# Gated linear attention and a tanh-shrink MLP: the first unit's scans chunk by chunk, and w_in fetched tile by tile

## The chip, the cores and the metric

The kernel runs on one core of a Trainium2 chip. Its time is the device time of one execution in microseconds (us); of several runs the median counts. Five engines work side by side, each through its own instructions in order: TensorE (PE; its weight loads are listed apart as PEld), VectorE (DVE), ScalarE (ACT), GpSimd (POOL) and SyncE (SP), whose queue issues nearly all of the transfers here.

## The reference

```python
# q, k, v, alpha: (4, 8, 768, 48) float32, alpha in 0.8..1
state = np.zeros((B, H, D, D))
for t in range(S):
    state = alpha[:, :, t, :, None] * state + np.einsum('bhd,bhe->bhde', k[:, :, t], v[:, :, t])
    y[:, :, t] = np.einsum('bhd,bhde->bhe', q[:, :, t], state)
x = y.transpose(0, 2, 1, 3).reshape(3072, 384)
h = x @ w_in               # (384, 2048), float64
g = h - np.tanh(h)
out = g @ w_out            # (2048, 384), float64
```

The two weights are float64, 6.3 MB each.

## The kernel before

**Units and chunks.** Tokens are worked in 12 units of 256 (three for each of the four batches), a unit in two chunks of 128. The recurrence is taken in closed form inside a chunk: a scan U of the decays from the chunk's end backwards and a scan W forwards (lines 703 to 724) turn k into `kU` and q into `qW`, so that `scores` is a plain matmul (line 775), `masked` keeps its causal half (799), `products` multiplies with v and adds what the state carried over (831), and `features` copies the result to `xT` (866). `decay`, `back`, `natural`, `update` and `state` carry the state to the next chunk. In a unit's tiles the free dimension is laid out as blocks of 128 tokens plus one zero column, so one scan runs over all eight blocks (four head pairs times two chunks, 1032 columns) and starts afresh at each.

**Transposed inputs.** Channels have to lie on partitions. For unit 0 all of alpha, k and q, and for unit 1 k and q, are transposed by matmuls with the identity (`turn`, 648): `rough` is the loaded tile, `turned` the result in PSUM. Half a holds the even tokens, half b the odd ones; `place` (672) copies alpha's halves to `aT`, a on ACT and b on DVE, while `times` (675) multiplies k by U and q by W straight from PSUM. Later units are transposed on DVE (`flip`).

**PSUM.** There are eight banks: one tile of two banks named `sc` (`two_banks`, 530), two of one bank in `ps_h`, and four in `ps_o`. Before the change unit 0's alpha is turned into `sc`, k into two of `ps_o`, q into the two of `ps_h`. Unit 0's scores go to `sc` for chunk 0 and to the two of `ps_h` for chunk 1. A tile whose buffer is used again waits until all readers of its former contents are through.

**MLP.** Each unit runs eight steps. `first` is 12 matmuls of `w_in` with `xT` to `h`; ACT and DVE form g from it; `second` multiplies with `w_out`. Units 0 and 1 do it plainly (8 matmuls of 384 columns, line 1051); from unit 2 on seven products take the place of eight, on sums of the weights' blocks that `combine` makes once all weights are there (line 1066).

**Weights.** `w_in` and `w_out` come in eight pieces each of 768 KB (`fetch`, 548; `load_weight`, 39; `weight_parts`, 47) into a pool of four `raw` buffers, and are rounded there: two passes on ACT (lines 83 and 84), two on DVE (86 and 87). A piece of w_out is one transfer to 128 partitions. A piece of w_in has three row tiles j, and its rows are placed in four groups of partitions: 0 to 47, 64 to 111, and the 16-row groups 48 to 63 and 112 to 127. Each group is one transfer for all three j: 288, 288, 96 and 96 KB. Later every piece is read a second time, for a check of its range (`reload` and `look`, 977 and 980), through the same function.

**Order.** The order on each engine is not written by hand. `Planner` (319) lists the tasks with an estimated time, a rank and the tasks they follow, simulates several orders, and emits the best one. Every task in a `go`, `go_c` or `add` call is such an entry; its third argument is the estimate. SP's queue is one of the planned engines, so a transfer that has to wait holds up all those behind it. TensorE's free time up to `y 0.0` is filled with idle matmuls (`spin`, 1124).

Of the kernel before, what the change touches and what calls it, by code (L numbers as in the profile page):

```python
# [9 lines left out]
FP32 = mybir.dt.float32  # L10
# [7 lines left out]
P = 128  # L18
# [20 lines left out]
def load_weight(nc, pool, rows, **kw):  # L39

    raw = pool.tile([P, WN], I64 if rows[0][1].dtype != FP32 else FP32, name="raw", **kw)
    for at, src in rows:
        nc.sync.dma_start(out=raw[at].rearrange("p (j n) -> p j n", n=src.shape[-1]), in_=src)  # L43
    return raw


def weight_parts(w_in, w_out, pad_rows, what, s):

    if what == "out":
        return [(slice(0, P), w_out.rearrange("(j p) n -> p j n", p=P)[:, 2 * s:2 * s + 2, :])]  # L50
    parts = []
    for i in range(len(pad_rows[0])):
        at, f0 = pad_rows[0][i]
        step = pad_rows[1][i][1] - f0
        src = w_in[f0:f0 + len(pad_rows) * step].rearrange("(j p) n -> p j n", p=step)
        parts.append((at, src[0:at.stop - at.start, :, 2 * s * P:2 * (s + 1) * P]))
    return parts

# [363 lines left out]
def fast(tc, q, k, v, alpha, moe_w_in, moe_w_out, out, w_in, w_out, ident, ok, pad_rows):  # L422
# [17 lines left out]
    with ExitStack() as ctx:  # L440
# [165 lines left out]
        def gla(u, rank):  # L606
# [5 lines left out]
            m = {}  # L612

            direct = u == 0

# [5 lines left out]
            for what, name in enumerate(("aT", "kT", "qT", "v")):  # L621
                go(f"load {name}", "SP", 1.3 if direct or u == 1 and by_matmul(u, what) else 2.0, -9 + 0.1 * what,
                   [what < 3 and u > 0 and not by_matmul(u - 1, what) and not by_matmul(u, what) and f"{name}{prev}"]
                   + [u == 1 and (f"kUb 0" if what == 3 else "turn qTb 0")]
                   + [f"{last} {u - 2}.{CU - 1}" for last in ("y", "state") if what == 3 and u > 1
                      and (last == "y" or (u - 2) % UPB < UPB - 1)],
                   lambda what=what: load(u, what), lat=2.5)
# [15 lines left out]
            def new(name):  # L643
                m[name] = two.tile([P, NP, CU, P], FP32, name=name)
                return m[name]
            makes = (lambda: tail[:, :, 0:P].rearrange("p (g c) t -> p g c t", c=CU),
                     lambda: new("kT"), lambda: new("qT"))
            def turn(what, n):

                if what == (2 if u else 0):  # L650
                    if "both" not in m:
                        m["both"] = two_banks()
                    t = m["both"][:, n]
                elif what == 2:
                    t = ps_h.tile([P, NP, P], FP32, name="turned", tag="h")
                else:
                    t = ps_o.tile([P, NP, P], FP32, name="turned", tag=f"o{2 * u + n}")
                m["turned", what, n] = t
                for g in range(NP):
                    for r in range(2):  # L660
                        at = (head(g, r) * CU + n) * D
                        T.matmul(t[HP * r:HP * r + HP, g, :], lhsT=rough[u, what][:, at:at + HP], rhs=ident,
                                 start=True, stop=True)

            def turned(what, n):
                return m.pop(("turned", what, n)).rearrange("p g (c i) -> p g c i", c=CU)

            def each(x, n):

                return x.rearrange("p (g c) (i two) -> p g c i two", c=CU, two=2)[:, :, :, :, n]  # L670

            def place(n):
                (V.tensor_copy if n else A.copy)(each(tail[:, :, 0:P], n), turned(0, n))

            def times(what, by, n):
                name = ("aT", "kT", "qT")[what]
                if n == 0:
                    new(name)
                V.tensor_mul(each(m[name].rearrange("p g c t -> p (g c) t"), n), turned(what, n), each(m[by][:, :, 1:], n))

            later = u > 0
            for n, ab in enumerate("ab"):
                if by_matmul(u, 0):
                    go(f"turn aT{ab}", "PE", 1.1, n * 0.1, ["load aT", later and "masked 0.0"], lambda n=n: turn(0, n))
                    go(f"aT{ab}", "DVE" if n else "ACT", 0.65, 0, [f"turn aT{ab}"], lambda n=n: place(n))
                if by_matmul(u, 1):
                    go(f"turn kT{ab}", "PE", 1.1, 1 + n * 0.1,
                       ["load kT"] + [later and x for x in ("x 0.0", "y 0.1", "state 0.1")], lambda n=n: turn(1, n))
                    go(f"kU{ab}", "DVE", 0.72, 3, [f"turn kT{ab}", "U", n and "kUa", later and "back 0.1", later and "turn qTb"],
                       lambda n=n: times(1, "U", n))  # L690
                if by_matmul(u, 2):
                    go(f"turn qT{ab}", "PE", 1.1, 2 + n * 0.1,
                       ["load qT", later and f"aT{ab}" if by_matmul(u, 0) else "masked 0.0"], lambda n=n: turn(2, n))
                    go(f"qW{ab}", "DVE", 0.72, 5, [f"turn qT{ab}", "W", n and "qWa", later and "y 0.1", later and "turn kTb"],
                       lambda n=n: times(2, "W", n))
            for what, (name, k_) in enumerate((("aT", 0), ("kT", 2), ("qT", 4))):
# [5 lines left out]

            def scan_U():


                U = m["U"] = two.tile([P, N, P + 1], FP32, name="U", bufs=1)
                V.tensor_tensor_scan(out=U.rearrange("p n t -> p (n t)")[:, ::-1], data0=aT[:, :0:-1],  # L707
                                     data1=after[:, ::-1], initial=0.0, op0=ALU.mult, op1=ALU.add)

            def ends():  # L710
                U = m["U"]
                e = m["ends"] = two.tile([P, NP, CU], FP32, name="ends")
                e = e.rearrange("p g c -> p (g c)")
                V.tensor_tensor(out=e, in0=U[:, :, 0], in1=low, op=ALU.max)
                V.reciprocal(before[:, 0::P + 1], e)

            def shortest():
                V.tensor_reduce(out=least[:, u:u + 1], in_=m["U"][:, :, 0], axis=AX.X, op=ALU.min)

            def scan_W():  # L720

                W = m["W"] = two.tile([P, N, P + 1], FP32, name="W", bufs=1)
                V.tensor_tensor_scan(out=W.rearrange("p n t -> p (n t)"), data0=aT[:, 0:N * (P + 1)],  # L723
                                     data1=before, initial=0.0, op0=ALU.mult, op1=ALU.add)

# [13 lines left out]
            def done(by, what):  # L739

                return lambda u: [f"{by}{ab} {u}" for ab in "ab"] if by_matmul(u, what) else [f"{by} {u}"]
            kU, qW = done("kU", 1), done("qW", 2)
            go("U", "DVE", 2.3, 1, (["aTa", "aTb"] if by_matmul(u, 0) else ["aT"])
               + (kU(u - 1) + [f"sizeU{prev}", f"least{prev}"] if prev else []), scan_U)
            go("ends", "DVE", 0.4, 3, ["U"], ends)
            go("least", "DVE", 0.15, 7, ["U"], shortest)
            go("W", "DVE", 2.3, 3, ["ends"] + (qW(u - 1) + [f"sizeW{prev}"] if prev else []), scan_W)
            if not by_matmul(u, 1):
                go("kU", "DVE", 1.4 if halved(u) else 1.2, 3, ["kT", "U"], lambda: scale("kT", "U"))
            if not by_matmul(u, 2):  # L750
                go("qW", "DVE", 1.2, 5, ["qT", "W"], lambda: scale("qT", "W"))
            go("sizeU", "ACT", 1.3, 5, ["U"], lambda: size("U", 0))
            go("sizeW", "ACT", 1.3, 7, ["W"], lambda: size("W", 1))

# [8 lines left out]
            def chunk(c):  # L763
# [56 lines left out]
                def decay():  # L820
                    V.tensor_mul(old[0:ROWS, :, 0:D], old[0:ROWS, :, 0:D],
                                 m["ends"][0:ROWS, :, c:c + 1].to_broadcast([ROWS, NP, D]))

# [84 lines left out]
                if past and not (u == 0 and c == 1):  # L908
                    held = [f"masked {past}"]
                    if u > PLAIN or u == PLAIN and c:  # L910
                        held += [f"x {past}", not past_last and f"state {past}", not last and "natural"]
                go_c("scores", "PE", 1.0 if halved(u) else 1.2, 7, kU(u) + qW(u) + held, scores)
                go_c("masked", "DVE", 1.55 if halved(u) else 1.4, 8, ["scores", f"y 0.0" if u == 1 and c == 0 else past and u > 0 and f"y {past}"], masked)
                if n > 0:
                    go_c("decay", "DVE", 0.4, 6, [f"ends {u}", f"state {past}"], decay)
                if direct:
# [5 lines left out]
                if not last:  # L922
                    go_c("back", "PE", 0.5, 6, kU(u) + [past and not past_last and f"state {past}", u > 0 and c and f"x {past}",
                                                       u > PLAIN and f"x {past}", u == PLAIN and not c and f"masked {past}"], back)
# [309 lines left out]
```

## Time and profile before

| | |
|---|---|
| median of 6 runs | 592.37 us (591.69 to 599.26) |
| profiled execution | 598.15 us; its span 596.4 us, 1.75 us outside it |
| mean granted TensorE clock | 0.996 |
| TensorE busy | 575.6 us (97%), 6.9 of it idle matmuls before 18 us |
| DVE, ACT busy | 443.2 (74%), 321.8 us (54%) |
| first MLP matmul | at 27.78 us |
| first matmul of the seven-product form | near 143.7 us |
| bytes moved | 50.68 MB, about 16.7 of them in the first 74.6 us (five slices of 14.9 us at 189, 182, 228, 234 and 284 GB/s) |

Times inside the profile count from the span's start. Averages over the whole span mislead here: the first tenth is short of data, the rest is nearly solid TensorE work, so what a change does to the first 75 us and to the few later gaps decides.

### The profile page before, as it was taken

To read this page: it belongs to the slowest core of one execution; us is meant where nothing else is said; L and a number is where in the kernel's file an instruction comes from. 1 tells how busy PE (TensorE), PEld (TensorE's weight loads), DVE (VectorE), ACT (ScalarE), POOL (GpSimd) and SP (SyncE) were. 2 spreads that over 40 slices of the span, in tenths; PEclk is the share of its full clock that TensorE was granted. 3 is DMA by queue.
4 is the path that set the end of the run, shared out by engine and by line. 5 is a ranking of instruction groups with operands and counts; after the bars stand their busy time and mean duration, and the time that the engine had idled before them with its cause. 6 is when DMAs were issued, how large, how long until landed. Compare 5 with 4: busy or idle time off the path is not lost.

```text
span 596.4 us, 11389 instructions
## 1 busy us (share of the span) xinstructions
PE 575.6 (97%) x4431; PEld 505.5 (85%) x4431; DVE 443.2 (74%) x860; ACT 321.8 (54%) x565; POOL 5.8 (1%) x22
## 2 busy tenths in 40 slices
PE   7988899999998999999999999999999999999994
PEld 7876677778997989889899898898999898899994
DVE  5977689989866968968788788868678745634642
ACT  2576897637747657566666454445443333423430
POOL 3000000000000000000000000000000000000000
PEclk9999999999999999999999999999999999999998
DMA  9999952126465472546242131130010000000001
GB/s 189 182 228 234 284 113 71 36 60 161 82 130 138 96 178 82 111 119 145 82 119 81 35 78 29 36 78 28 27 35 1 27 8 1 29 8 0 27 0 34
DMA packets 60831, 50.68 MB, mean 85 GB/s; under 512 B 35904, under 2 KB 50528, under 8 KB 60768
## 3 DMA queue, kind: packets, MB, share of 16 engines
q1 hardware_dynamic: 57856, 48.88, 35.5%
q10 hardware_dynamic: 2912, 0.98, 0.8%
q8 instruction: 37, 0.61, 0.4%
q14 instruction: 26, 0.21, 0.1%
HBM read 44.04 MB, written 4.72 MB: 82 GB/s over the span
## 4 chain that ended last, share of the span: by engine, by line
PE 75%; DMA 13%; DVE 3%; ACT 3%; SPq 2%; issue 2%; ACTq 0%; DVEq 0%
PE h L1006 34%; PE o L1066 26%; PE o L1051 6%; DMA raw<-in_moe_w_in_dram 5%; PE sc L858 3%; DMA ar<-in_alpha_dram 3%; PE sc L796 3%; DMA vt<-in_v_dram 2%; PE sc L846 2%; DMA kr<-in_k_dram 1%; DMA raw<-in_moe_w_out_dram 1%; PE sc L897 1%; DMA qr<-in_q_dram 1%; PE sc L884 1%; SPq L43 1%
## 5 line engine op out<-in xcount | busy, mean ns | idle before, releaser
L1006 PE MATMUL h<-xT,w_in 128*128 128x256 f32 x1152 | 265.7, 380 | 2.3 <-DVE w_in L87 1.7
L1006 PEld LDWEIGHTS h<-xT,w_in 128*128 128x128 f32 x1152 | 215.0, 190 | 30.7 <-DVE w_in L87 2.1
L1015 ACT ACTIVATE u<-h 128x512 f32<-128x512 f32 x96 | 56.9, 593 | 167.5 <-PE h L1006 167.2
L1023 DVE TENSOR_TENSOR w<-h,u 128x512 f32<-128x512 f32 x96 | 66.0, 688 | 92.1 <-ACT u L1015 91.0
L1066 PE MATMUL o<-b,e 128*128 128x192 f32 x480 | 91.1, 326 | 0.0
L1066 PE MATMUL o<-w_out,e 128*128 128x192 f32 x320 | 81.2, 336 | 0.0
L1066 PEld LDWEIGHTS o<-b,e 128*128 128x128 f32 x480 | 80.2, 190 | 0.0
L1027 DVE SCALAR_TENSOR_TENSOR g<-z,w 128x512 f32<-128x512 f32 x96 | 65.7, 686 | 9.0 <-ACT z L1019 5.2
L1066 PE MATMUL o<-b,g 128*128 128x192 f32 x320 | 65.1, 326 | 0.0
L1019 ACT ACTIVATE z<-u 128x512 f32<-128x512 f32 x96 | 60.2, 628 | 2.3
L1066 PEld LDWEIGHTS o<-w_out,e 128*128 128x128 f32 x320 | 56.0, 190 | 4.6 <-issue 0.5
L1066 PEld LDWEIGHTS o<-b,g 128*128 128x128 f32 x320 | 54.2, 190 | 0.0
L1033 ACT ACTIVATE big<-u 128x1024 f32<-128x1024 f32 x48 | 50.3, 1048 | 0.1
L1051 PE MATMUL o<-w_out,g 128*128 128x384 f32 x128 | 44.3, 489 | 2.8 <-DVE g L1027 1.8
L1051 PEld LDWEIGHTS o<-w_out,g 128*128 128x128 f32 x128 | 23.9, 190 | 16.9 <-DVE g L1027 2.2
L1039 DVE TENSOR_TENSOR e<-g 128x256 f32<-128x256 f32 x80 | 33.3, 416 | 1.6
L1040 DVE TENSOR_TENSOR e<-g 128x256 f32<-128x256 f32 x80 | 33.2, 415 | 0.0
L818 DVE TENSOR_TENSOR pm<-sc,mask 64x256 f32<-64x256 f32 (+1 forms) x60 | 28.7, 505 | 3.3 <-PE sc L796 3.0
L707 DVE TENSOR_TENSOR_SCAN U<-aT,after 128x1032 f32<-128x1032 f32 x12 | 27.5, 2293 | 0.1
L723 DVE TENSOR_TENSOR_SCAN W<-aT,before 128x1032 f32<-128x1032 f32 x12 | 27.6, 2298 | 0.0
L83 ACT ACTIVATE more<-raw 128x768 int16<-128x768 uint32 x16 | 17.2, 1076 | 15.1 <-DMA raw<-in_moe_w_in_dram 9.0
L796 PEld LDWEIGHTS sc<-qT,kT 48*64 48x64 f32 x640 | 15.2, 133 | 9.6 <-issue 4.3
(126 smaller groups left out, 549.1 us busy)
## 6 DMA issues: line engine op xcount, KB each, us to landing
raw<-in_moe_w_out_dram SPq DMA_DIRECT2D x16, 768.0 KB, 6.4
raw<-in_moe_w_in_dram SPq DMA_DIRECT2D x32, 288.0 KB, 6.2
ar<-in_alpha_dram SPq DMA_DIRECT2D x44, 96.0 KB, 3.1
kr<-in_k_dram SPq DMA_DIRECT2D x40, 96.0 KB, 2.3
qr<-in_q_dram SPq DMA_DIRECT2D x40, 96.0 KB, 2.2
raw<-in_moe_w_in_dram SPq DMA_DIRECT2D x32, 96.0 KB, 5.8
vt<-in_v_dram SPq DMA_DIRECT2D x20, 96.0 KB, 2.6
vt<-in_v_dram SPq DMA_DIRECT2D x40, 48.0 KB, 2.6
```

The costliest lines, as they stand in the source:

```text
L796: T.matmul(sc[r][rows:rows + HP, g, HP * half:], lhsT=m["kT"][q, g, c, rows:rows + HP], rhs=m["qT"][q, g, c, HP * half:], start=True, stop ...
L818: V.tensor_mul(to, of, mask[rows, gs, ts].unsqueeze(1).to_broadcast(list(to.shape)))
L1006: T.matmul(h[:, a, :], lhsT=w_in[:, j, f * P:(f + 1) * P], rhs=xT[u][:, j, :], start=(j == 0), stop=(j == KT - 1))
L1015: A.activation(m["u", s], m["h", s], AF.Square, scale=W_SCALE ** -1.5)
L1019: A.activation(m["z", s], m["u", s], AF.Square, bias=QB, scale=QA * W_SCALE)
L1023: V.tensor_mul(m["w", s], m["h", s], m["u", s])
L1027: V.scalar_tensor_tensor(out=g.rearrange("p a c t -> p (a c t)"), in0=m["z", s], scalar=QK, in1=m["w", s], op0=ALU.add, op1=ALU.mult)
L1033: A.activation(big, m["us", s // 2].rearrange("p s t -> p (s t)"), AF.Relu, bias=-U_FAST, scale=W_SCALE, accum_out=over[:, n:n + 1])
L1039: V.tensor_add(e[:, 0:2, :], g[:, 0], g[:, 1])
L1040: V.tensor_sub(e[:, 2:4, :], g[:, :, 1, :], g[:, :, 0, :])
L1051: T.matmul(m["o"][c], lhsT=g[:, a, c, :], rhs=w_out[:, f, :], start=(f == 0), stop=(f == FT - 1))
L1066: T.matmul(o[n][:, i], lhsT=g_, rhs=w_, start=(s == 0 and (n, i) in ((0, 0), (1, 0), (2, 1), (3, 0))), stop=(s == FS - 1), skip_group_chec ...
```

## The change

**Scans by chunk, in unit 0 only.** `aT`, U, W, kT and qT lay their blocks chunk first (`gc`). Each of U, `ends` and W becomes two tasks, one for each chunk with half the columns, and each of `kU` and `qW` becomes four: half a or b of the tokens, chunk a or b. The scores of chunk 0 are listed after chunk a's parts alone. Units 1 to 11 keep one scan for both chunks.

**Banks.** Unit 0's alpha is turned into two single banks of `ps_o`, k into the two of `ps_h`, q into `sc`.

**Pieces of w_in.** The transfers to 48 partitions are cut by row tile: 0 to 47 and 64 to 111 for j = 0, the same for j = 1, for j = 2, and then the two 16-row transfers with all three j. That makes eight transfers of 96 KB for a piece, where there were four. It holds for the fetch and for the reload. The planner's estimates for these tasks stay as they were (4.1 and 1.0 us on SP).

```diff
-        parts.append((at, src[0:at.stop - at.start, :, 2 * s * P:2 * (s + 1) * P]))
-    return parts
+        src = src[0:at.stop - at.start, :, 2 * s * P:2 * (s + 1) * P]
+        few = at.stop - at.start < 32
+        parts += [(0, at, slice(0, len(pad_rows)), src)] if few else [(j - 9, at, slice(j, j + 1), src[:, j:j + 1]) for j in range(len(pad_rows))]
+    return [x[1:] for x in sorted(parts, key=lambda x: (x[0], x[1].start))]
...
+            parted = u == 0
+            parts = [(x, slice(c * NP, (c + 1) * NP), slice(c, c + 1)) for c, x in enumerate("ab")] if parted else [("", slice(0, N), slice(0, CU))]
...
-                if what == (2 if u else 0):
+                if what == 2:
                     t = m["both"][:, n]
-                elif what == 2:
+                elif what == 1 and u == 0:
                     t = ps_h.tile([P, NP, P], FP32, name="turned", tag="h")
                 else:
                     t = ps_o.tile([P, NP, P], FP32, name="turned", tag=f"o{2 * u + n}")
...
-                    go(f"kU{ab}", "DVE", 0.72, 3, [f"turn kT{ab}", "U", ...
+                    for x, _, cs in parts:
+                        go(f"kU{ab}{x}", "DVE", 0.42 if x else 0.72, 3, [f"turn kT{ab}", f"U{x}", ...
...
-            def scan_U():
+            def scan_U(ns):
+                a, z = ns.start * (P + 1), ns.stop * (P + 1)
+                V.tensor_tensor_scan(out=m["U"][:, ns].rearrange("p n t -> p (n t)")[:, ::-1], data0=aT[:, z:a:-1],
+                                     data1=after[:, a:z][:, ::-1], initial=0.0, op0=ALU.mult, op1=ALU.add)
...
+            for x, ns, _ in parts:
+                go(f"U{x}", "DVE", 1.2 if x else 2.3, 1, (["aTa", "aTb"] if by_matmul(u, 0) else ["aT"]) ...
+                go(f"ends{x}", "DVE", 0.4, 3, [f"U{x}"], lambda ns=ns: ends(ns))
+                go(f"W{x}", "DVE", 1.2 if x else 2.3, 3, [f"ends{x}"] + ...
...
-                go_c("scores", "PE", 1.0 if halved(u) else 1.2, 7, kU(u) + qW(u) + held, scores)
+                go_c("scores", "PE", 1.0 if halved(u) else 1.2, 7, kU(u, c) + qW(u, c) + held, scores)
```

## The prediction

> **What bounds the kernel now.** I read the page's engine shares and slices first, then a table of stretches, TensorE's waits, the chain up to 70 us, and the instructions of the first 30 us.
>
> ```profile
> PE 575.6 (97%) x4431; PEld 505.5 (85%) x4431; DVE 443.2 (74%) x860; ACT 321.8 (54%) x565; POOL 5.8 (1%) x22
> DMA  9999952126465472546242131130010000000001
> ```
>
> TensorE is the bound of the whole, but the transfer engines are full for the first five slices (75 us). A change helps only where TensorE stands still.
>
> ```profile
> 30.00:40.00 10.00, 9.35 (x81) 7.28 (x82) 7.20 (x13) 6.79 (x10) 0.00 (x0) 1.00 1.04 214
> 40.00:50.00 10.00, 7.12 (x65) 5.02 (x66) 6.09 (x11) 8.79 (x13) 0.00 (x0) 1.00 1.07 246
> ...
> 60.00:70.00 10.00, 8.18 (x32) 5.66 (x31) 6.57 (x10) 8.44 (x12) 0.00 (x0) 1.00 1.04 305
> ```
>
> Columns: stretch, length, busy us of PE, PEld, DVE, ACT, POOL, granted clock, transfer share, GB/s. TensorE loses 0.65 + 2.88 + 1.82 = 5.35 us here, with transfers at 1.04 or more. Its waits by name:
>
> ```profile
> PE o L1051 <- DVE g L1027: 1.8, 1, 1.8
> PE h L1006 <- DVE w_in L87: 1.7, 1, 1.7
> PE o L1051 <- DVE w_out L87: 1.0, 1, 1.0
> PE h L1006 <- DVE w L1023: 0.6, 1, 0.6
> ```
>
> Those are 5.1 of the 5.35 us. 2.7 wait for a rounded weight outright; the 1.8 (at 66.18) stand behind a rounding too, as the chain shows:
>
> ```profile
> 13.01 6.48 DMA raw<-in_moe_w_in_dram
> ...
> 22.28 7.45 DMA raw<-in_moe_w_in_dram
> ...
> 32.73 9.99 DMA raw<-in_moe_w_in_dram
> ...
> 43.23 10.84 DMA ar<-in_alpha_dram
> ...
> 54.14 8.32 DMA raw<-in_moe_w_out_dram
> ...
> 63.49 1.05 ACT more L84
> ```
>
> From 13 to 63 us one transfer releases the next: SP issues only when an earlier one has landed. By the issues' own landings it is always the eighth before (issue 13.90, landing 13.88; 14.26, 14.23; 40.41, 40.40; 41.62, 41.60). Eight are in flight at most, so the rate of the transfers sets the pace.
>
> Later gaps are 1.95 us (180 to 200), 1.29 (220 to 240) and 1.05 (240 to 280). The end from 280 us is solid.
>
> **Part 1, alpha's banks.**
>
> ```profile
> 8.61 0.64 ACT L673 COPY aT<-sc 128x512 f32<-128x512 f32 x1 [3.58 <-PE sc L662]
> 9.28 0.69 DVE L673 COPY aT<-sc 128x512 f32<-128x512 f32 x1 [4.50 <-ACT aT L673]
> ```
>
> The turns of both halves take 5.56 to 8.50; ACT's copy of half a starts only after both, DVE's of b after ACT's. With a bank each, a can be copied after its own 16 matmuls, 7.0 (half of the 2.94 us) to 7.9, and ends by 8.6. So b starts at 8.6, whether or not it still waits for a: 0.7 us off DVE's start of U.
>
> **Part 2, scans by chunk.** DVE works without a break from 9.28 to the end of chunk 1's mask at 21.8 (including 1.5 us for rounding w_in's first piece, 17.85 to 19.40). Extra instructions in unit 0: one scan more for U and for W, two for `ends` (0.16 + 0.20 us), two products more each for kU and qW. The halves of the 2.30 us scan cost 0.06 (smallest memset) to 0.2 more each: 0.1 to 0.4. A product of 256 columns starts every 0.34 us (L1039) where one of 512 starts every 0.61: 4 x (0.68 - 0.61) = 0.3; by the 0.505 us of the mask's 256 columns from PSUM against 0.675 it is 4 x 0.335 = 1.3. `ends` adds 0.36. Sum 0.8 to 2.1; I take 1.0, since L1039 is the same shape.
>
> What it should buy is chunk 0's scores before chunk 1's scans. But q's turned halves now lie in `sc`, which has one buffer, and scores 0.0 goes to `sc`: it waits for chunk 1's qW after all. The four scans, `ends`, kU and qW, about 8.5 us of DVE, therefore come first: 9.28 - 0.7 + 8.5 + the extra, near 18, as now (17.94). Then masks, TensorE's products (y 0.1 ends at 25.2) and the first MLP matmul follow as before. So part 1 and 2 together: -0.7 + 1.0 = +0.3, and -1.5 if w_in's rounding falls behind the masks, where it is hidden by y 0.1. Bounds -1.9 (with extra 0.3) to +1.4; I take -0.4.
>
> **Part 3, the pieces.** Price of an issue: median 0.426 us, so a w_in piece costs SP 8 x 0.43 = 3.4 instead of 1.7 us; eight fetches add 13.6 us before 68 us, eight reloads as much up to 270. Behind them in SP's queue stand w_out's fetches, unit 1's k, q and v and later alpha, k, q. Closing entries of a transfer are 4-byte packets of 18 ns: 64 more a piece over 16 engines is 0.1 us.
>
> What it may gain is the rate. The packet records before 70 us: w_in's 2 KB packets take 182 ns (median), w_out's 3 KB packets 142, and w_out alone (65.7 to 67.6) runs at 400 GB/s. In the undisturbed reload of 147.86 the 48-row transfers land at 151.94 and 153.73: 295 KB in 1.79 us, 165 GB/s. Its first hundred packets take about 90 ns, then 170 to 240. So w_in is slow by where its rows lie, in SBUF or in HBM; the trace can't say which. Upper and lower rows in turn help if it is SBUF's side, and not if it is HBM's stride.
>
> [...]
>
> Bounds by rows: no gain (a piece spans 5.5 to 6.6 us early), or 3.4 us, where issuing becomes the limit (98 KB each 0.426 us is 231 GB/s); a w_out piece takes 2.0. I take 4, nearer the second, since 96 KB transfers of q land 2.0 us after issue on an idle queue (200.52 to 202.53), well within the 3.4 us that eight in flight allow. Fetch pairs start every (58.49 - 36.62)/3 = 7.3 us now and about 5.5 to 6 then, so by the sixth pair weights come some 8 us early. TensorE can't use more than it loses, 5.35. Next late is ACT, which rounds (2.1 us a piece) and makes u and z: busy 8.79 and 8.44 of ten us already. I take 3.2 of 5.35; bounds 0 and 5.35.
>
> In the reload the last landing comes 6.9 us after the first issue (147.86 to 154.73); then 7 x 0.43 + 2.0 to 2.2, near 5.2. What is queued behind is issued 1.7 us later but shares the engines with less. The later gaps (4.3 us) wait on such loads, through ACT: I take 0, bounds -2 and +3.
>
> **Sum.** -0.4 - 3.2 + 0 = -3.6 us: 598.15 becomes 594.55 for the profiled execution. That execution lies 5.8 above the median of the runs; taking the difference over, 592.37 - 3.6 = 588.8. This likeliest case spans 585.5 to 591.
>
> **Rivals.** *The transfers open up wholly:* all 5.35 us, rounding behind the masks (-1.9), and 1 to 2 of the later gaps: -8.3 to -9.3, 583 to 584. For it: the chain from 13 to 63 us is transfers alone. Against it: ACT's 8.79, and an order planned by estimates that the change leaves alone. 0.22.
>
> *Part 3 does not do what it says:* the rate is HBM's, 2 KB rows at a pitch of 16 KB; only -0.4 +- 1.5 is left, 590.5 to 593.5. For it: the 16-row transfers, on far fewer partitions, land 0.57 and 0.43 us apart, 172 to 228 GB/s, not slower. Against it: those overlap with the wide ones' end. 0.16.
>
> *Slower: the eight in flight.* A w_in piece now fills all eight places by itself, where two pieces and a w_out fitted. If a piece still takes 5.9 us, and w_out's 2.0 no longer overlap, the pair takes 7.9, with one landing (2.0) laid bare 9.3 instead of 7.3: 5 to 16 us later over eight pairs, of which TensorE's plain steps, tied to each piece, lose about 7: 599. It decides once a pair takes over 7.3 us. For it: the loaded queue makes even 96 KB take 10.84 us (43.23). Against it: that transfer stood behind two w_out pieces. 0.12.
>
> **How the numbers follow.** Forecast 0.50, rivals 0.22, 0.16 and 0.12. A measurement can tell about 1% from no change: 586.4 and 598.3. Below 586.4 lie the first rival and 0.08 of the forecast's own 0.50: 0.30. Above 598.3 lies most of the last, 0.09. The rest is 0.61. The range 583.5 to 593 leaves out a third of the first rival and nearly all of the last, about 0.19.
>
> **What would show it.** In the changed profile: DVE's copy of alpha at 8.6; scores 0.0 after the last qW, near 18; w_in packets near 100 to 130 ns instead of 182 and pairs every 5.5 to 6 us; TensorE's waits for `w_in L87` and `w_out L87` mostly gone before 66 us, ACT at 9 of ten there. Wrong would be: packets still at 180 ns, scores 0.0 well before 17 us, or new TensorE gaps behind late k, q or alpha after 130 us, where SP's queue is longer.

## The result and the profile after

| | before | after |
|---|---|---|
| median of the runs | 595.20 us (83 runs, 590.29 to 602.21) | 592.98 us (41 runs, 590.92 to 596.46) |
| ratio, 95% interval | | 0.9973 [0.9961, 0.9986] |
| profiled run, its span | 598.15, 596.4 us | 591.46, 589.6 us |
| first MLP matmul | 27.78 us | 27.77 us |
| TensorE idle, 20 to 70 us | 5.35 us | 1.62 us |

The change makes the kernel 0.27% faster, 1.6 us; 3.6 us, 0.6%, was forecast. The ratio is that of the means, over the fast runs of each kernel alone (those within 1.5% of its fastest, 76 of the 83 and all 41), so it is not the quotient of the two medians. The median of the kernel before moved too, from 592.37 us in the six runs shown to 595.20 in 83, so the ratio counts and not the difference from 592.37. The two profiled runs are 6.7 us apart, three times the difference of the medians: one execution each says little about a difference of this size.

First the page of the changed kernel: TensorE's line of busy times, then the transfers' share in 40 slices.

```profile
PE 573.4 (97%) x4425; PEld 504.3 (86%) x4425; DVE 443.4 (75%) x868; ACT 321.9 (55%) x565; POOL 5.8 (1%) x22
DMA  8899852043463433443342120220010000000001
```

TensorE's work is the same. The transfers are no longer full in the first slices. The stretches of ten microseconds, in the columns explained in the prediction:

```profile
30.00:40.00 10.00, 8.78 (x71) 7.25 (x71) 8.33 (x14) 8.59 (x13) 0.00 (x0) 1.00 0.90 220
40.00:50.00 10.00, 9.74 (x102) 7.34 (x100) 9.21 (x16) 8.60 (x14) 0.00 (x0) 1.00 1.01 282
...
60.00:70.00 10.00, 10.00 (x40) 7.41 (x39) 8.29 (x14) 9.24 (x14) 0.00 (x0) 1.00 0.95 320
```

The holes of 2.88 us (40 to 50) and 1.82 us (60 to 70) have shrunk to 0.26 and 0. The stretch from 30 to 40 got worse, 1.22 us for 0.65, and ScalarE (ACT) is at 8.6 to 9.2 of ten. TensorE's waits, each with its total, number and longest:

```profile
PE sc L816 <- ACT kn L908: 2.4, 2, 1.8
...
PE sc L808 <- DVE qT L687: 1.5, 1, 1.5
PE h L1026 <- DVE w L1043: 1.2, 1, 1.2
...
PE h L1026 <- DVE w_in L90: 0.3, 1, 0.3
```

Waits for a rounded weight fell from 2.7 us to 0.3. What is left stands behind ACT: `kn` and, through `u`, `w`. The chain shows the same (start, length, what):

```profile
21.39 5.59 DMA raw<-in_moe_w_in_dram
...
29.02 2.84 DMA raw<-in_moe_w_in_dram
...
32.92 1.05 ACT more L87
33.98 1.00 ACT junk L752 x2
34.98 0.48 ACT u L1035
...
39.45 3.54 DMA raw<-in_moe_w_in_dram
...
50.67 2.79 PE h L1026 x12
```

Before, transfers led the chain until 63 us. Now the last one in this part ends at 43, and from 46 us the chain is TensorE's own. Between 32.9 and 35.5 three passes of ACT stand in it one behind another; they matter below.

The start, from the instructions of ACT, DVE and TensorE:

```profile
6.95 0.63 ACT L678 COPY aT<-turned 128x512 f32<-128x512 f32 x1 [1.92 <-PE turned L671]
7.84 0.70 DVE L678 COPY aT<-turned 128x512 f32<-128x512 f32 x1 [3.06 <-PE turned L671]
16.46 1.16 PE L808 MATMUL sc<-qT,kT 48*128 48x128 f32 x16 [1.53 <-DVE qT L687]
```

DVE takes its half of alpha up when TensorE has turned it, no longer after ACT: 1.44 us earlier. The first scores still wait for chunk 1's last qW, as forecast, and start 1.5 us earlier than before. Nothing of this is left at 27.77, the first MLP matmul.

### The profile page after: what moved, and what is told of

Read it like the earlier page. It is cut to its first block, busy times and chain, and to the rows that moved or that the text cites. A ratio compares the mean times of both kernels' runs of the same rounds, so it can differ in the third digit from the quotient of the medians.

```text
span 589.6 us, 11492 instructions
## 1 busy us (share of the span) xinstructions
PE 573.4 (97%) x4425; PEld 504.3 (86%) x4425; DVE 443.4 (75%) x868; ACT 321.9 (55%) x565; POOL 5.8 (1%) x22
## 4 chain that ended last, share of the span: by engine, by line
PE 82%; DMA 5%; DVE 5%; ACT 4%; issue 2%; SPq 1%; POOL 0%; ACTq 0%; DVEq 0%; POOLq 0%
PE h L1026 37%; PE o L1086 27%; PE o L1071 7%; PE sc L878 3%; PE sc L816 3%; DMA raw<-in_moe_w_in_dram 2%; PE sc L866 2%; DMA ar<-in_alpha_dram 1%; PE sc L917 1%; DVE U L719 1%; PE sc L904 1%; DMA vt<-in_v_dram 1%; PE spin L1148 1%; ACT u L1035 1%; ACT junk L752 1%
## 5 line engine op out<-in xcount | busy, mean ns | idle before, releaser
L738 DVE TENSOR_TENSOR_SCAN W<-aT,before 128x1032 f32<-128x1032 f32 (+1 forms) x13 | 27.7, 2133 | 0.0
L719 DVE TENSOR_TENSOR_SCAN U<-aT,after 128x1032 f32<-128x1032 f32 (+1 forms) x13 | 27.6, 2133 | 0.1
L639 ACT COPY ar<-ar 32x512 f32<-32x512 f32 x22 | 13.5, 616 | 21.0 <-DMA ar<-in_alpha_dram 13.4
```

Of the source, the lines that this page charges most:

```text
L719: V.tensor_tensor_scan(out=m["U"][:, ns].rearrange("p n t -> p (n t)")[:, ::-1], data0=aT[:, z:a:-1], data1=after[:, a:z][:, ::-1], initia ...
```

## The experiments

They ran in three batches, each on one chip beside 35 runs of the kernel before (medians 595.83, 597.09 and 594.45 us). Ratios go against the batch's own; medians are of 12 runs. The two repeats of the kernel before, as a load of its own, show what ratios can tell:

**The kernel before, again (batches 1 and 3).** No edit.

> The kernel before, unchanged, as its own control: ratio 1.000 with an interval of about 0.002 to each side. Its profile is a second execution of the same program. If the 6.8 us between the two profiled spans (596.4 and 589.6) were all the change's, this span is near 596; if much of it is the scatter of executions (590.3 to 602.2 us before), the span lies elsewhere, and the trace shows at which time from the start the two executions of one program part.

> The kernel before as its own control, a second time: by chance alone 1.000 within 0.002. Together with the first control (0.9978) it tells how far a ratio here can be off through the load of the program, beyond its interval.

Measured: 593.84 us, 0.9978 [0.9952, 1.0003], and 596.02 us, 1.0007 [0.9972, 1.0043]. Two loads of one program have differed by 0.2% from the runs beside them. TensorE's idle time from 20 to 70 us was 3.75 and 4.01 us: the 5.35 of the profile that the prediction started from is the highest of three.

**The changed kernel, again (batches 2 and 3).** No edit.

> The changed kernel, unchanged. Its profile gives a second execution. Reading so far: in every profile a stretch of 3.41 us in which TensorE stood still for 1.97 us or more was followed by one at half clock (1.7 us lost), and none with 1.60 or less; and the changed kernel's median granted clock over its runs (0.993 to 0.994) is lower than that of the kernel before (0.996). Theory (the changed order gathers TensorE's slack in the gaps near 35 and 213 us, and these cost clock in part of the executions): median clock 0.992 to 0.995 again, below that of before on the same chip, and where this profile shows half clock away from the end, it follows the gap near 35 or near 213 us. At equal clock the kernel is 3 to 4 us faster than before, in the median 1.5 to 3: ratio 0.995 to 0.998. Rival (the clock is scatter and tells nothing): same median clock as before.

> The changed kernel, a third time. Its ratio has been 0.9973 and 0.9933. Theory: median clock 0.992 to 0.995, ratio 0.993 to 0.998; half clock in the profile, if any, after the gap near 35 or near 214 us.

Measured: 593.68 us, 0.9933 [0.9902, 0.9964], and 592.77 us, 0.9943 [0.9917, 0.9970]. With 0.9973 that makes a gain of 0.3 to 0.7% in three measurements: the sign holds in each, but the size moves by 0.4 points, somewhat more than between the repeats above (0.3). The median clocks, 0.993 and 0.9945, are as expected and below those of the kernel before in the same batches (0.995 and 0.996); the ratio of 0.9933 is a little below the 0.995 to 0.998 expected of it. In the first of the two profiles the clock falls after the gaps near 35 and 214 us, after stretches with 1.54 and 1.75 us of idle time, less than the 1.97 read until then; in the second it does not fall inside the work.

**Pieces alone, and the scans and banks alone (batch 1).** The first is the kernel before with the changed `load_weight` and `weight_parts`, the second the changed kernel with the old two:

```diff
...
-        parts.append((at, src[0:at.stop - at.start, :, 2 * s * P:2 * (s + 1) * P]))
-    return parts
+        src = src[0:at.stop - at.start, :, 2 * s * P:2 * (s + 1) * P]
+        few = at.stop - at.start < 32
+        parts += [(0, at, slice(0, len(pad_rows)), src)] if few else [(j - 9, at, slice(j, j + 1), src[:, j:j + 1]) for j in range(len(pad_rows))]
+    return [x[1:] for x in sorted(parts, key=lambda x: (x[0], x[1].start))]
```

> The kernel before with part 3 alone: w_in's pieces in eight transfers, upper and lower rows in turn. The planner's order is that of before. Theory (all of the gain is the pieces' rate, and TensorE's wait between 20 and 70 us is what it can buy): packets of w_in near 115 ns instead of 182, TensorE's lost time from 20 to 70 us from 5.35 to about 1.6 us, as in the changed kernel, and a ratio of 0.994 to 0.998. Rival (the scans and the new order bring the gain): ratio 0.999 to 1.002 though the packets are fast. Rival (the pieces gain more and the new order gives some back): ratio under 0.994.

> The changed kernel with w_in's pieces as before: parts 1 and 2 alone, in the changed planner's order. Theory (all of the gain is the pieces'): packets at 180 ns, y 0.1 ends about 1 us earlier than 25.2, first MLP matmul still near 27.8, ratio 0.999 to 1.001. Rival (scans and order bring the gain): ratio 0.996 to 0.998. Rival (they give some back): ratio 1.002 to 1.005.

Measured: 593.73 us, 0.9950 [0.9917, 0.9983], and 595.50 us, 0.9984 [0.9948, 1.0019]. The pieces alone give what the whole change gives, with 2.16 us of idle time from 20 to 70 (1.6 expected); the scans and banks give nothing that can be told from the repeats. What the scans and banks do when weights come slowly is seen in the second kernel's stretches:

```profile
30.00:40.00 10.00, 6.52 (x42) 5.47 (x41) 6.35 (x12) 7.93 (x12) 0.00 (x0) 0.95 1.01 207
40.00:50.00 10.00, 10.00 (x89) 7.45 (x88) 7.60 (x14) 8.92 (x14) 0.00 (x0) 0.88 1.06 235
```

The holes at 40 and 60 us are gone, and one of 3.48 us stands near 35: the planned order asks for the first MLP step's `w` sooner, and it comes later. Right behind it the granted clock falls to 0.95 and 0.88 (of the stretch).

**The same eight transfers, not in turn (batch 1).** The kernel of the pieces alone, with the same sizes, the same number of issues and the same rows of HBM; the three upper transfers first, then the three lower:

```diff
-[(j - 9, at, slice(j, j + 1), ...
+[(at.start - 999, at, slice(j, j + 1), ...
```

> As the pieces alone, with eight transfers of 96 KB, but the three of the upper rows first and then the three of the lower ones. Size, number of issues and the stride in HBM are those of the pieces alone; only the turn is missing. If the rate is limited by which rows of SBUF are written at one time: packets stay near 170 to 180 ns, a piece spans 5 to 6.5 us, ratio 1.000 to 1.006 (the extra issues cost and nothing is gained). If it was the size of a transfer, or the stride in HBM, that made them slow: packets near 115 ns and the ratio of the pieces alone.

Measured: 599.71 us, 1.0062 [1.0032, 1.0092]. The median of w_in's 2 KB packets before 70 us was 182 ns before (180 and 168 in its repeats), 196 with the old pieces under the new scans, 160 here, and 113 (changed) and 127 (pieces alone) in turn; in all nine profiles with the turn it is 109 to 127. So the smaller transfer explains less here (182 to 160 ns) than the turn of upper and lower rows of SBUF (160 to 127). Its stretches:

```profile
40.00:50.00 10.00, 6.93 (x57) 4.70 (x54) 5.90 (x10) 7.74 (x13) 0.00 (x0) 0.95 1.01 221
180.00:200.00 20.00, 17.03 (x133) 14.49 (x126) 14.00 (x30) 14.22 (x27) 0.00 (x0) 0.83 0.52 133
```

TensorE idles 3.07 us from 40 to 50 and 2.97 in one stop near 187, and the granted clock is down to 0.95 and 0.83 of these stretches. Against the pieces in turn, which differ in nothing else, this kernel is 1.1% slower. Against the kernel before it is 3.7 us slower, but not because its weights come later: w_in's eighth piece lands at 65.7 us (65.6, 64.3 and 63.6 in three profiles of before), and TensorE's idle time from 20 us on is 8.2 us (9.6, 6.3 and 7.6 before). What differs is the clock: 0.9909 by the mean of its 12 runs, 0.9955 in the 35 of the kernel before beside them. Of 594 us that difference is 2.7 us by estimate, most of the 3.7.

**Pieces and banks (batches 2 and 3).** Pieces, and the bank mapping, on the kernel before; scans whole, the planner's order of before:

```diff
-                if what == (2 if u else 0):
+                if what == 2:
...
-                elif what == 2:
+                elif what == 1 and u == 0:
```

> The kernel before with the pieces and the banks, without the scans by chunk; the planner's order is that of before. By the theory that the new order costs clock and the pieces give the time: median clock as before (0.996), alpha's copy on DVE at 7.9 to 8.6 instead of 9.28, ratio 0.993 to 0.996, below the changed kernel on the same chip. Rival (the scans by chunk are worth their cost): ratio above that of the changed kernel by 0.001 or more.

> The pieces and the banks in the order of before, once more. Two loads of one program have differed by 0.002 here, so this shows whether 0.992 holds: by the theory (pieces 3 to 4 us, no clock lost) 0.991 to 0.996 and a median clock of 0.996 or more, not above the changed kernel on the same chip.

Measured: 593.08 us, 0.9919 [0.9891, 0.9948], and 594.11 us, 0.9981 [0.9945, 1.0017]. Beside the changed kernel in the same batches (593.68 and 592.77) it is once 0.6 us less, once 1.3 more: no difference. The cut of the scans can't be seen in the time. The second load missed what was expected of it in all three points: the ratio is above 0.996, the median clock 0.9945, and it is slower than the changed kernel beside it. Its interval holds 1, so by itself it shows no gain.

**The scores' bank set free (batch 2).** The changed kernel, with unit 0's alpha and q turned into `ps_h` and k into `ps_o`, so that scores 0.0 need not wait for chunk 1's qW:

```diff
-                if what == 2:
+                if what == 2 and u > 0:
...
-                elif what == 1 and u == 0:
+                elif what != 1 and u == 0:
```

> The changed kernel, but unit 0's q is turned into the two banks of ps_h (after alpha, which goes there too) and k into two of ps_o, so that sc is free for chunk 0's scores. Same planner's order. If q's halves in sc hold chunk 0's scores back, as the prediction said: scores 0.0 start near 15.2 instead of 16.46 us and the gap of 1.53 us before them goes, y 0.1 ends about 1 us earlier than 24.3. Theory on the total: the plain steps wait for weights and for DVE near 35 us anyhow, so little of that 1 us reaches the end: ratio within 0.002 of the changed kernel on the same chip. Rival (the start sets the end): 0.002 lower.

Measured: 593.19 us, 0.9947 [0.9919, 0.9975], no more than the change itself. TensorE's instructions with a wait:

```profile
15.90 1.16 PE L808 MATMUL sc<-qT,kT 48*128 48x128 f32 x16 [0.19 <-DVE qT L687]
25.21 0.66 PE L671 MATMUL turned<-ident,rough 128*64 128x128 f32 x8 [0.55 <-DMA rough<-in_k_dram]
26.34 1.53 PE L671 MATMUL turned<-ident,rough 128*64 128x128 f32 x24 [0.48 <-DMA rough<-in_k_dram]
38.94 1.62 PE L1026 MATMUL h<-xT,w_in 128*128 128x256 f32 x3 [3.33 <-DVE w L1043]
```

The wait of 1.53 us is gone, and scores 0.0 starts at 15.90, 0.56 us earlier than in the changed kernel and not the 1.3 expected; y 0.1 ends 0.55 earlier (23.79). The next thing is late at once: unit 1's k arrives 1.03 us after TensorE wants it, the first MLP matmul comes at 28.68 and not at 27.77, and the wait for `w` near 35 us grows to 3.33.

**Eight idle matmuls near 35 us (batch 2).** The changed kernel, with TensorE kept at work ahead of the gap near 35 us:

```diff
+                    if u == 0 and s == 2:
+                        warm = ps_o.tile([P, P], FP32, name="warm", tag="o0")
+                        for _ in range(8):
+                            T.matmul(warm, lhsT=ident, rhs=ident, start=True, stop=True)
```

> The changed kernel with eight idle matmuls (about 1.1 us) into an unused bank ahead of unit 0's third first step, where TensorE stands still near 35 us. They add nothing to the output. If that gap costs clock in part of the executions: median clock up by 0.001 to 0.002, time down by 0.5 to 1.5 us against the changed kernel on the same chip. If the half clock comes from the gap near 213 us alone, or the clock tells nothing: no difference, within 0.001.

Measured: 593.05 us, 0.9929 [0.9903, 0.9955]. In the profile the full clock was kept near 35 us, where a gap of 1.28 us is left (another of 1.01 near 25 waits for unit 1's k), but it was lost for 3.41 us after a gap of 2.26 near 216. The median clock is 0.9955, for 0.993 of the changed kernel beside it, and 6 of 12 runs reach 0.996, for 2 of 12: the clock rose as expected, and a little more. The time, 593.05 for 593.68, is lower by as much as expected (0.5 to 1.5), but that is within the scatter of 12 runs: the gain is not shown, and one gap of two was covered.

**Reload in four transfers (batch 3).** Pieces and banks, with the eight transfers in the fetch alone:

```diff
...
-        few = at.stop - at.start < 32
+        few = whole or at.stop - at.start < 32
...
-    return [x[1:] for x in sorted(parts, key=lambda x: (x[0], x[1].start))]
+    return [x[1:] for x in sorted(parts, key=lambda x: (x[0], x[1].stop - x[1].start < 32, x[1].start))]
...
-            looked[n] = load_weight(nc, combo_pool[0], weight_parts(moe_w_in, moe_w_out, pad_rows, *pieces[n]))
+            looked[n] = load_weight(nc, combo_pool[0], weight_parts(moe_w_in, moe_w_out, pad_rows, *pieces[n], whole=True))
```

> The pieces and the banks in the order of before, but the second reading of the weights in four transfers a piece, as before. Prediction's step: the second reading was put at 0 with bounds -2 and +3 us. If that holds, the ratio is that of the pieces and banks on the same chip within 0.002, and TensorE's gaps from 180 to 270 us are as large as with eight (1.65, 0.97 and 0.96 us). If SP's eight issues delay the loads behind them: lower by 0.002 to 0.005, gaps smaller. If the faster second reading helps: higher by as much.

Measured: 595.01 us, 1.0005 [0.9973, 1.0037], against 0.9981 with both: within the scatter of a repeat, so the reload's share is not settled beyond that. The later gaps, 1.44, 0.57 and 0.78 us, are smaller than with eight transfers, though the ratio is higher: the two signs point to different rivals. A lone reload lands 6.1 us after its first issue in the changed kernel (146.62 to 152.69), 6.9 before; 5.2 was forecast.

## Why the forecast was half wrong

The forecast time, 588.8 us, is 4.2 below the 592.98 measured, and 2.8 of that is the base: 592.37 was the median of six runs, 595.20 is that of 83. That 592.98 still lies just inside the range of 583.5 to 593 is luck. What the theory has to answer for is the gain: 3.6 us forecast, 1.6 measured here, 4.0 and 3.4 by the ratios of the two repeats.

**The mechanism of part 3 was right.** Packets of 113 ns were in the band of 100 to 130; a piece takes 4.3 to 5.3 us from its first packet to its last (4 forecast, 5.4 to 6.7 before); waits for a rounded weight are nearly gone, and ACT is at nine of ten, as forecast. Too hopeful was the pace: from the third w_in piece to the eighth, last landings come every 6.5 us ((60.8 - 28.5)/5) where it was 7.2 ((65.6 - 29.7)/5), not 5.5 to 6 (the other profiles: 7.0 and 6.6 after, 7.0 and 6.9 before). The eighth comes at 60.8, 63.1 and 61.3 us in the three profiles of after, at 65.6, 64.3 and 63.6 in the three of before: 2.8 us early by the means, not 8. That was still enough to close the holes at 40 and 60 us.

The kernel not in turn shows what the turn does: with the same transfers and the same rows of HBM, w_in's packets take 160 ns without it and 127 with it, and the ratio goes from 1.0062 to 0.9950. In turn, 16 engines with 2 KB each 113 ns make 290 GB/s by the median packet, 182 ns 180 GB/s. What in the writing of these rows sets the rate, no run shows.

**The term that failed is the sum's "-3.2 of 5.35, later gaps 0".** It took one execution's idle time as the kernel's, and a gap's price as its length. Both are off. In its place the runs show 2.9 us of 4.37 before 70 us and 0.7 in the later gaps, and against them a lost clock worth about 1.1 us:

*The idle time did fall by about the sum.* From 20 us to its last matmul TensorE stood still for 9.6, 6.3 and 7.6 us in the three profiles of before (5.35, 3.75 and 4.01 of it before 70 us), and for 4.5, 4.7 and 3.6 in three of after. By the means that is 3.6 us less, the very sum of the forecast, but partly by luck: its terms were -0.4, -3.2 and 0, and what came is nothing at the start, 2.9 us before 70 us (4.37 to 1.51) and 0.7 in the later gaps.

*But the gaps that are left can take the clock with them, as in the second profile of after.* No step of the prediction had the clock in it. This is that profile in stretches of 3.41 us:

```profile
33.21:36.62 3.41, 1.87 (x22) 1.45 (x20) 1.83 (x3) 3.38 (x6) 0.00 (x0) 1.00 1.05 200
36.62:40.03 3.41, 3.06 (x7) 2.52 (x8) 2.73 (x6) 3.41 (x7) 0.00 (x0) 0.50 0.54 152
214.11:217.53 3.42, 1.67 (x37) 1.18 (x35) 2.75 (x2) 3.32 (x8) 0.00 (x0) 1.00 0.64 197
217.53:220.94 3.41, 3.41 (x12) 3.41 (x12) 3.37 (x8) 3.41 (x7) 0.00 (x0) 0.50 0.13 35
```

In the first and third TensorE stands still for 1.54 and 1.75 us; in the stretch after each the granted clock is half, for 3.41 us, at a cost of 1.7 us of work by estimate, half of the 3.41. The matmuls show it: twelve that take 2.6 to 2.8 us elsewhere take 4.34 here.

```profile
36.97 4.34 PE L1026 MATMUL h<-xT,w_in 128*128 128x256 f32 x12 [1.89 <-DVE w L1043]
```

All nine falls of the clock inside the work, in all 14 profiles, start at a multiple of 3.41 us from the clock's first rise, right after a stretch of that length with 1.54 to 2.72 us of idle time (eight of them 1.73 or more); two go on for a second stretch. No stretch with 1.73 us or more was passed without a fall, but six with 1.55 to 1.65 were (the repeat of before, one after the other):

```profile
62.92:66.33 3.41, 1.81 (x7) 1.09 (x7) 2.63 (x4) 2.90 (x6) 0.00 (x0) 1.00 1.03 366
66.33:69.75 3.42, 3.42 (x16) 2.74 (x15) 2.90 (x4) 3.42 (x8) 0.00 (x0) 1.00 1.03 399
```

What else decides between 1.54 and 1.65 is open. A gap that lay across two stretches stayed harmless: the first profile of after has one of 1.79 us that ends at 215.09, split into 0.89 and 0.90, and keeps its clock; the second has 1.75 in one and loses it. The stretches began elsewhere in each execution (the first rise comes at 4.69 to 7.70 us in the 14 profiles); that this scatters the runs is not shown.

*The new order makes such gaps likelier.* Near 35 us the second profile of after has these on ACT and DVE:

```profile
32.62 1.10 ACT L86 ACTIVATE more<-raw 128x768 int16<-128x768 uint32 x1 [2.21 <-DVE kT L687]
33.57 1.04 ACT L87 ACTIVATE more<-raw 128x768 f16<-128x768 f32 x1
34.48 1.04 ACT L752 ACTIVATE junk<-W 128x1032 f32<-128x1032 f32 x1
...
35.51 0.58 ACT L1035 ACTIVATE u<-h 128x512 f32<-128x512 f32 x1
...
36.13 0.69 DVE L1043 TENSOR_TENSOR w<-h,u 128x512 f32<-128x512 f32 x1 [1.42 <-ACT u L1035]
```

The `h` that `u` reads is done at 31.01, but `u` is queued behind two rounding passes and the measuring pass `junk`, 2.9 us; `w` and the next matmuls wait. And the first of these passes waits itself, 2.21 us with ACT idle: it rounds w_in's fourth piece, which lands at 32.5. (The line names `kT`, which ends at the same time; in the first profile of after it names the transfer.)

```profile
31.97 1.09 ACT L86 ACTIVATE more<-raw 128x768 int16<-128x768 uint32 x1 [1.38 <-DMA raw<-in_moe_w_in_dram]
```

So the gap follows that piece: with its rounding begun at 31.63, 31.97, 32.62, 34.05 and 34.62 us, in the three profiles of the changed kernel and in two variants (the scans and banks alone, the free bank), it is 0.41, 1.22, 1.89, 3.48 and 3.33 us. In the order of before `u` stands ahead of the fourth piece's rounding, and the gap is 0.65 us in each of eight profiles, however late the piece comes:

```profile
32.74 0.58 ACT L1015 ACTIVATE u<-h 128x512 f32<-128x512 f32 x1
...
36.31 1.08 ACT L83 ACTIVATE more<-raw 128x768 int16<-128x768 uint32 x1 [1.92 <-DVE w_in L87]
```

The clock fell inside the work in four of six profiles with the changed order, in two of eight with the order of before. The prediction named ACT as the next late thing, and priced what it can't deliver, but neither that the new order ties TensorE to a transfer through ACT's queue nor what the gap does to the clock.

The runs bear it out, without proving it. In the 67 runs of the changed kernel the mean granted clock is 0.9935; in the 129 runs of the kernel before in the three batches it is 0.9954 (by batches 2 and 3 alone, where both ran side by side, 0.9931 and 0.9952). Each of these holds 5.0 to 7.6 us at half clock behind TensorE's last matmul, as the 14 profiles have them, which cost no work. A difference of 0.0019 is 1.1 us of 594, so 3.6 less idle time leaves 2.5; the pooled medians differ by 2.8 (592.92 and 595.76). Among runs with a clock of 0.996 or more the medians are 591.47 (0.21 of the runs) and 594.64 (0.56): 3.2 us. Pieces and banks, in the order of before, reach that clock in 0.50 of their 24 runs. They are no faster for it, and their profiles show why: TensorE stands still for 6.4 and 6.9 us from 20 us on, where the changed kernel has 4.3 by the mean, so what they keep of the clock they lose in idle time. That the lost clock takes about a third of the gain is an estimate from these runs; the one kernel meant to remove it covered one gap of two, and raised the clock without a measurable gain. Why the first measurement gives 1.6 us and the repeats 4.0 and 3.4 stays open; two loads of the kernel before differ by 0.3% (0.9978 and 1.0007), 1.7 us, and two of pieces and banks by 0.6%.

**Part 1 and 2 (-0.4) came to nothing in the time**, within the bounds. DVE's copy came at 7.84, not 8.6, because the turns into two banks took 2.10 us (5.64 to 7.74) where I had used the 2.94 of before. A half scan takes 1.22 us, 0.07 more than half of 2.30, as estimated. The extra instructions were put too high: from alpha's copy to the last qW DVE takes 8.6 us (7.84 to 16.41) where it took 8.4 (9.28 to 17.66). With a reduction of 0.14 us that no longer lies between, they cost some 0.3 us. The sum took 1.0 and put the least at 0.8, while the bound of -1.9 took 0.3 without saying from what. The case of -1.5 came true, too: w_in's first piece is rounded at 24.87, behind the masks, where it was 17.85. But y 0.1 ends only 0.9 us earlier (24.34 for 25.2), and between it and the first MLP matmul stand 3.4 us of unit 1's turns, 2.6 before: the gain was filled with work that the order put there.

**Rivals.** HBM's stride is out (160 against 127 ns with the same rows). The transfers did not open up wholly: 4.5 us of gaps remain. The slower rival comes near the time of the kernel not in turn (599 and 599.71) by luck. Its price was 7 us over the kernel before, and 3.7 were measured; its pair of pieces was to take 9.3 us, and there they come every 7.3, for 6.9 to 7.2 before. That loss went mostly through the clock, as the means of the runs show.

No version beat the changed kernel: pieces and banks, the free bank and the idle matmuls all lie between 593.05 and 594.11.

## What to carry to other kernels

Before cutting a transfer, look at which rows of SBUF it writes: narrow transfers to different halves, issued in turn, took 109 to 127 ns a packet here for 168 to 196, and the same cut without the turn made the kernel slower (1.0062). Price a gap of TensorE with the clock behind it: here 1.54 us in one stretch of 3.41 was followed by half clock for 3.41 us, and twelve matmuls took 4.34 us for 2.6 to 2.8. Where the gain is a few microseconds of idle time, take it from several profiles of before, and look at which engine becomes late next, what it has queued ahead of the short instruction that everyone waits for, and whether that waits for a transfer.

## What the runs showed of the hardware

In the 14 profiles all nine falls of the granted clock inside the work came at multiples of 3.41 us from its first rise: after every such stretch with 1.73 us or more of idle TensorE time (up to 2.72) and after one with 1.54, while six with 1.55 to 1.65 were passed; the prediction had no term for stops so short. And a single profile's gaps vary by over a microsecond and a half between executions of one program (5.35, 3.75 and 4.01 us).
